# The transform's fp32 matmuls as two column tiles, the filter's as row tiles, and the filter's sums four channels at a time

## The chip, the cores and the metric

The kernel runs on one core of a Trainium2 chip. The metric is the device time of one execution in microseconds (us), lower is better. TensorE (PE) multiplies, and loads its stationary operands through a path that the profile lists as PEld; VectorE (DVE), ScalarE (ACT) and GpSimd (POOL) do the elementwise work, and SyncE (SP) issues most transfers.

## The reference

```python
h_mlp  = np.maximum(pos_emb @ w1, 0.0) @ w2            # (12480, 64) -> (12480, 128)
h_filt = h_mlp * np.exp(-0.01 * pos)[:, None]
Uf = np.fft.rfft(x * v, n=2 * S, axis=1)               # x, v: (2, 12480, 128)
Hf = np.fft.rfft(h_filt, n=2 * S, axis=0)
y  = np.fft.irfft(Uf * Hf[None], n=2 * S, axis=1)[:, :S]
x  = (x * y).reshape(24960, 128)
h = x @ w_in;  x = (h * np.cos(h)) @ w_out             # 128 -> 2048 -> 128
h = x @ w2_in; out = (h * np.clip(h + 3, 0, 6) / 6) @ w2_out
```

A long convolution with a filter that a small network makes from positions, then two wide layers in a row. Everything is fp32.

## The kernel before, in words

All work of a core stands in the order in which the code is written; nothing reorders it but the semaphores.

**Filter.** The 114 columns of positions are handled as two halves (`M2` = 57) stacked on the partitions: rows 0 to 63 hold the first half's features, rows 64 to 127 the second's. `mlp(k)` multiplies a chunk of four columns by a block-diagonal `w1b` (fp32) into `rp`; ACT makes its ReLU `rh` rounded to fp32r, DVE the rest `rl`. `filt(k)` multiplies each column with a block-diagonal `w2` in three fp32r products (`rh`·`w2h`, `rh`·`w2l`, `rl`·`w2h`) of 256 columns into `hps`; ACT copies a part of it (`raw`) for POOL, and POOL and DVE multiply by the window into `h`. There are 15 chunks.

**Transform.** The convolution of length 111 × 113 is done two channels at a time (`CH`), 64 iterations of the loop over `i`. A stage `s1(i, g)` multiplies 4 stationary blocks of 121 columns (two kinds, at columns 0 to 56 and 64 to 120, `OD` = 64) with the 112 columns of `f1` into `ap`; group 0 and 1 are the two batches' `uf`, group 2 the filter's `hf`. Two ACT copies (L269, L270) bring it to `at`: the lower half as it is, the upper half with its two parts exchanged. `s2h` and `s2u` (`xh`, `xp`) finish the forward transform, DVE multiplies (`pq`, `y`), `s2i` (`bp`) and `s1i` (`v`) go back, DVE forms `w`, and `fin` on POOL makes `z`, which is stored to DRAM. Each iteration of the loop holds stages of several `i`. For one `i + 2` POOL also makes `q` and, in `make_hf`, one product `hm` and four small sums (`hf`), for which the filter `h` lies in SBUF.

**The two layers** (`moe_phase`) run after the convolution with fp32r matmuls of 512 columns; a decoder in the loop prepares their weights.

An fp32 matmul of the code appears in the trace as two records, each with a weight load of its own; an fp32r matmul as one.

Of the kernel before, what the change touches and what calls it, by code (L numbers as in the profile page):

```python
# [22 lines left out]
R = 64  # L23
# [20 lines left out]
def kernel(  # L44
# [109 lines left out]
    def conv_phase(cctx):  # L154
# [18 lines left out]
        uf = [const.tile([N1, B, 2, CH, 128], FP32, name=f"uf{k}") for k in range(2)]  # L173
        hf = [const.tile([N1, 2, CH, 128], FP32, name=f"hf{k}") for k in range(2)]
        for k in range(2):
# [46 lines left out]
        def make_u(i, parts=(0, 1, 2)):  # L222
# [8 lines left out]
            for part, o, op in ((1, 0, ALU.add), (2, OD, ALU.subtract)):  # L231
                if part in parts:
                    nc.vector.tensor_tensor(out=f[:, :, o:o + M2], in0=pf, in1=qf, op=op)

        def make_hf(i):
            if i >= NG:
                return
            hm = p_u.tile([N1, CH, MP], FP32, tag="hm", name="hm")
            h = h_of(i * CH, CH)

            def sums(s_, t):
                for o, op in ((0, ALU.add), (OD, ALU.subtract)):
                    nc.gpsimd.tensor_tensor(
                        out=hf[i % 2][:, s_, :, o:o + M2], in0=t[:, :, :M2], in1=t[:, :, M2:], op=op
                    )

            if i < 2:
                sums(0, h)
            nc.gpsimd.tensor_tensor(
                out=hm, in0=h, in1=sig[:N1].unsqueeze(1).to_broadcast([N1, CH, MP]), op=ALU.mult  # L250
            )
            if i >= 2:
                sums(0, h)
            sums(1, hm)


        def s1(i, g, pool=None):
            if i >= NG:
                return
            if i not in a_t:  # L260
                a_t[i] = p_2.tile([KE, 2, 12, K1], FP32, tag="at", name="at")
            at = a_t[i]
            ap = (pool or ps_a).tile([KE, 4, 2, K1], FP32, tag="a", name="ap")
            for q in range(4):
                s, c = divmod(q, CH)
                st = (uf[i % 2][:, g, s, c] if g < 2 else hf[i % 2][:, s, c])[:, :KE]
                nc.tensor.matmul(out=ap[:, q].rearrange("p z k -> p (z k)"), lhsT=st, rhs=f1)  # L267
            src = ap.rearrange("p q z k -> p z q k")
            nc.scalar.copy(at[:OD, :, 4 * g:4 * g + 4, :], src[:OD])  # L269
            nc.scalar.copy(at[OD:, ::-1, 4 * g:4 * g + 4, :], src[OD:])  # L270

        with ExitStack() as hctx:
            hp = hctx.enter_context(tc.tile_pool(name="hp", bufs=1))
            hr = hctx.enter_context(tc.tile_pool(name="hr", bufs=3))
# [18 lines left out]
            nc.vector.memset(idle, 0.0)  # L293
            busy = ps_a.tile([128, 4 * NP1], FP32, tag="a", name="busy")
            for _ in range(2):
# [7 lines left out]
            for k in range(2, 8):  # L303
                load_pos(k)
            nc.vector.tensor_copy(w2h, w2s)
            nc.vector.tensor_tensor(out=w2l, in0=w2s, in1=w2h, op=ALU.subtract)
            rt = {}

            def mlp(k):
                n = chunks[k][1]  # L310
                rp = ps_r.tile([128, CB, NP1], FP32, tag="rp", name="rp")
                nc.tensor.matmul(out=rp[:, :n], lhsT=w1b, rhs=pt.pop(k)[:, :n])
                rh = hr.tile([128, CB, NP1], F32R, tag="rh", name="rh")
                rl = hr.tile([128, CB, NP1], F32R, tag="rl", name="rl")
                nc.scalar.activation(out=rh[:, :n], in_=rp[:, :n], func=ACTF.Relu)
                nc.vector.scalar_tensor_tensor(
                    out=rl[:, :n], in0=rp[:, :n], scalar=0.0, in1=rh[:, :n], op0=ALU.max, op1=ALU.subtract
                )
                rt[k] = (rh, rl)

            def filt(k):
                c0, n = chunks[k]
                rh, rl = rt.pop(k)
                hps = ps_h.tile([N1, CB, 2, D], FP32, tag="hps", name="hps")
                raw = hr.tile([N1, CB, 2, D - HS[2]], FP32, tag="raw", name="raw")
# [3 lines left out]
                nc.scalar.copy(raw[:, :n], hps[:, :n, :, HS[2]:])  # L329
                for e in range(2):  # L330
                    m = n
                    j0 = e * M2 + c0
                    nc.gpsimd.tensor_tensor(
                        out=h_p[2][:, :, j0:j0 + m].rearrange("p d c -> p c d"),
                        in0=raw[:, :m, e],
                        in1=win[:, j0:j0 + m].unsqueeze(2).to_broadcast([N1, m, D - HS[2]]),
                        op=ALU.mult,
                    )
                    for q, t in enumerate(h_p[:2]):
                        nc.vector.tensor_tensor(  # L340
                            out=t[:, :, j0:j0 + m].rearrange("p d c -> p c d"),
                            in0=hps[:, :m, e, HS[q]:HS[q + 1]],
                            in1=win[:, j0:j0 + m].unsqueeze(2).to_broadcast([N1, m, HS[q + 1] - HS[q]]),
                            op=ALU.mult,
                        )
# [81 lines left out]
        def s2i(i, g, pool=None):  # L427
            if not 0 <= i < NG:
                return
            if i not in b_t:  # L430
                if i < NG - 1:
                    b_t[i] = p_2.tile([2 * K1, 8, MP], FP32, tag="b", name="b")
                else:
                    t = p_2.tile([KE, 2, 12, K1], FP32, tag="at", name="bz").rearrange("p z q k -> p (z q k)")
                    b_t[i] = t[:2 * K1, :8 * MP].rearrange("p (a b) -> p a b", b=MP)
            src = (pool or ps_a).tile([2 * K1, 4, MP], FP32, tag="a", name="bp")
            for q in range(4):
                nc.tensor.matmul(out=src[:, q, :], lhsT=y_t[i][:, 4 * g + q, :], rhs=f2)  # L438
# [27 lines left out]
        def s1i_of(i, b, pool, tag):  # L466
            v = pool.tile([NP1, 2, 4, M2], FP32, tag=tag, name="vb")
            for z in (1, 0):
                nc.tensor.matmul(out=v[:, z], lhsT=gm[:, z, :], rhs=b_t[i][:, 4 * b:4 * b + 4, z * M2:(z + 1) * M2])
            vs = p_1.tile([NP1, 4, M2], FP32, tag=f"v2s{b}", name="v2b", bufs=3)  # L470
# [32 lines left out]
        for i in range(NG):  # L503
# [43 lines left out]
        def s1i_3(b):  # L547
            for z in (1, 0):
                nc.tensor.matmul(
                    out=vv[z][:, 4 * b:4 * b + 4], lhsT=gm[:, z, :],  # L550
                    rhs=b_t[n - 3][:, 4 * b:4 * b + 4, z * M2:(z + 1) * M2],
                )
            vs = p_1.tile([NP1, 4, M2], FP32, tag=f"v2s{b}", name="v2b", bufs=3)
# [276 lines left out]
def _constants():  # L830
# [75 lines left out]
```

## Time and profile before

| what | us |
|---|---|
| median of 3 runs (2753.46 to 2754.5) | 2754.06 |
| the profiled execution | 2752.64 |
| its span, first to last instruction | 2750.8 |
| filter, 4.44 to 38.09 | 33.65 |
| start of the loop, 38.09 to 62.04 | 23.95 |
| loop, i = 3 to 62, 62.04 to 537.54 (60 iterations) | 475.50 |
| end of the loop, 537.54 to 557.83 | 20.29 |
| the two layers, 557.83 to 2750.80 | 2192.97 |

The stretches are cut at first matmuls of a kind; the profiled execution takes 1.84 us more than its span, which lies before and after the instructions. PE is busy for 2733.3 us of the span (99%), PEld for 2199.1 (80%), DVE for 2349.4 (85%), ACT for 2273.1 (83%) and POOL for 2435.7 (89%). A matmul's busy time is longer than the distance to the next one, because matmuls are pipelined; where a rate is wanted, read distances between starts.

### The profile page before, as it was taken

Reading aid. Unit: us, or ns where it says so; the run is one execution under the profiler, and the core shown is the slowest. Engines: PE = TensorE matmul, PEld = TensorE weight load, DVE = VectorE, ACT = ScalarE, POOL = GpSimd, SP = SyncE. Lnnn points to the kernel's source line nnn. Section 1 sums busy time; section 2 is a strip of 40 time slices with the busy share of each in tenths; the row PEclk is TensorE's granted clock in tenths of the full one; section 3 lists DMA queues with packets and bytes.
Section 4 is the critical chain, followed back from the end, with each engine's and each line's share of the span. In section 5 each row is a group of like instructions: output and inputs, shape, how many; then the busy total and the mean of one; then the engine's idle time right before and its main releaser. Section 6 shows DMA issues by size and latency. Waiting matters only on the chain.

```text
span 2750.8 us, 39540 instructions
## 1 busy us (share of the span) xinstructions
PE 2733.3 (99%) x12965; PEld 2199.1 (80%) x12965; DVE 2349.4 (85%) x3199; ACT 2273.1 (83%) x3286; POOL 2435.7 (89%) x1544
## 2 busy tenths in 40 slices
PE   9999999989999999999999999999999999999999
PEld 7777777768888888888888888888888888888888
DVE  7888888778888888888888888888888888888887
ACT  5878777688888888888888888888888888888885
POOL 6999999788898889888988889888988888888887
PEclk9999999999999999999999999999999999999999
DMA  3333332200000000000000000000000000000000
GB/s 114 98 101 97 95 104 81 58 27 8 16 8 16 8 16 16 8 16 8 16 8 16 9 16 8 16 9 16 15 9 16 8 16 8 16 8 16 8 8 12
DMA packets 88288, 79.49 MB, mean 29 GB/s; under 512 B 57139, under 2 KB 78870, under 8 KB 88086
## 3 DMA queue, kind: packets, MB, share of 16 engines
q1 hardware_dynamic: 87790, 76.77, 10.2%
q8 instruction: 106, 1.74, 0.3%
q14 instruction: 96, 0.79, 0.1%
q10 hardware_dynamic: 296, 0.20, 0.0%
HBM read 51.19 MB, written 25.74 MB: 28 GB/s over the span
## 4 chain that ended last, share of the span: by engine, by line
PE 97%; ACT 1%; POOL 0%; DVE 0%; issue 0%; DMA 0%; SPq 0%; DVEq 0%; ACTq 0%
PE acc L733 39%; PE hb L665 20%; PE ha L665 19%; PE ap L267 6%; PE bp L438 4%; PE v L446 3%; PE xp L385 3%; PE xh L385 2%; POOL lo L698 0%; ACT r L685 0%; ACT k L675 0%; DMA x<-z 0%; DVE g L686 0%; ACT hi L693 0%; DVE r L676 0%
## 5 line engine op out<-in xcount | busy, mean ns | idle before, releaser
L723 POOL TENSOR_TENSOR lo<-g,hi 128x1024 fp32r<-128x1024 f32 (+1 forms) x390 | 938.8, 2407 | 238.9 <-PE ha L665 159.0
L698 POOL TENSOR_TENSOR lo<-g,hi 128x1024 fp32r<-128x1024 f32 (+1 forms) x392 | 942.0, 2404 | 3.4 <-ACT hi L693 2.7
L675 ACT ACTIVATE k<-ha,biasq 128x512 int32<-128x512 f32 (+1 forms) x768 | 509.1, 689 | 293.0 <-PE ha L665 292.8
L686 DVE TENSOR_TENSOR g<-ha,r 128x512 f32<-128x512 f32 (+1 forms) x768 | 500.1, 690 | 284.1 <-ACT r L685 283.9
L665 PE MATMUL hb<-x2h,vi 128*128 128x512 f32 (+1 forms) x1564 | 549.8, 392 | 0.0
L665 PE MATMUL ha<-xh,wi 128*128 128x512 f32 (+1 forms) x1524 | 535.5, 392 | 3.1 <-DVE g L686 3.0
L685 ACT ACTIVATE r<-r,biaspi 128x512 f32<-128x512 f32 (+1 forms) x776 | 520.3, 719 | 0.1
L676 DVE SCALAR_TENSOR_TENSOR r<-k,ha 128x512 f32<-128x512 int32 (+1 forms) x768 | 488.9, 677 | 2.9 <-ACT k L675 2.0
L706 DVE SCALAR_TENSOR_TENSOR g<-q,hb 128x1024 f32<-128x1024 f32 (+1 forms) x391 | 472.5, 1208 | 8.1 <-ACT q L705 8.1
L720 DVE SCALAR_TENSOR_TENSOR hi<-q,hb 128x1024 fp32r<-128x1024 f32 (+1 forms) x390 | 470.0, 1205 | 0.0
L705 ACT ACTIVATE q<-hb,bias 128x1024 f32<-128x1024 f32 (+1 forms) x391 | 435.3, 1113 | 20.5 <-PE hb L665 16.9
L733 PE MATMUL acc<-hi,vo 128*128 128x512 f32 (+1 forms) x1568 | 428.2, 395 | 0.0
L733 PE MATMUL acc<-hi,wo 128*128 128x512 f32 (+1 forms) x1568 | 427.7, 394 | 0.0
L693 ACT CAST hi<-g 128x1024 fp32r<-128x1024 f32 (+1 forms) x385 | 399.7, 1038 | 0.0
L733 PEld LDWEIGHTS acc<-hi,wo 128*128 128x128 f32 x1568 | 294.9, 188 | 71.4
L733 PEld LDWEIGHTS acc<-hi,vo 128*128 128x128 f32 x1568 | 294.3, 188 | 68.5
L665 PEld LDWEIGHTS hb<-x2h,vi 128*128 128x128 f32 x1564 | 293.7, 188 | 69.0 <-issue 0.4
L665 PEld LDWEIGHTS ha<-xh,wi 128*128 128x128 f32 x1524 | 286.2, 188 | 71.4 <-issue 3.1
L665 PE MATMUL hb<-x2l,vi 128*128 128x512 f32 (+1 forms) x782 | 306.5, 392 | 0.0
L665 PE MATMUL ha<-xl,wi 128*128 128x512 f32 (+1 forms) x762 | 303.9, 399 | 0.0
L733 PE MATMUL acc<-lo,wo 128*128 128x512 f32 (+1 forms) x784 | 247.7, 397 | 0.6 <-POOL lo L698 0.2
L733 PE MATMUL acc<-lo,vo 128*128 128x512 f32 (+1 forms) x784 | 245.8, 394 | 0.0
(144 smaller groups left out, 3402.1 us busy)
## 6 DMA issues: line engine op xcount, KB each, us to landing
x<-in_x_dram SPq DMA_DIRECT2D x64, 199.5 KB
v<-in_v_dram SPq DMA_DIRECT2D x64, 199.5 KB
scr<-z SPq DMA_DIRECT2D x128, 98.9 KB
out_dram<-o SPq DMA_DIRECT2D x47, 256.0 KB
xf<-scr SPq DMA_DIRECT2D x17, 256.0 KB
wst<-in_wi_dram SPq DMA_DIRECT2D x8, 512.0 KB
wst<-in_wo_dram SPq DMA_DIRECT2D x8, 512.0 KB
pt<-in_post_dram SPq DMA_DIRECT2D x14, 224.0 KB
```

The source lines that it names most:

```text
L665: nc.tensor.matmul(out=hs[c][:, 0, :n], lhsT=w["i", e][:, sl], rhs=r[:, :n], start=(k == 0), stop=(k == 2))
L675: nc.scalar.activation(out=k[:, c, :n], in_=h, func=ACTF.Identity, bias=biasq, scale=1.0 / TWO_PI)
L676: nc.vector.scalar_tensor_tensor(out=un.r[:, c, :n], in0=k[:, c, :n], scalar=-TWO_PI, in1=h, op0=ALU.mult, op1=ALU.add)
L685: nc.scalar.activation(out=rc, in_=rc, func=ACTF.Sin, bias=biaspi, scale=1.0)
L686: nc.vector.tensor_tensor(out=un.g[:, c, :n], in0=h, in1=rc, op=ALU.mult)
L693: nc.scalar.copy(un.hi[:, :, :n], un.g[:, :, :n])
L698: nc.gpsimd.tensor_tensor(out=un.lo[:, :, :n], in0=un.g[:, :, :n], in1=un.hi[:, :, :n], op=ALU.subtract)
L705: nc.scalar.activation(out=un.r[:, c, :n], in_=h, func=ACTF.Relu, bias=bias3, scale=1.0)
L706: nc.vector.scalar_tensor_tensor(out=un.g[:, c, :n], in0=un.r[:, c, :n], scalar=6.0, in1=h, op0=ALU.min, op1=ALU.mult)
L720: nc.vector.scalar_tensor_tensor(out=un.hi[:, c, :n], in0=un.r[:, c, :n], scalar=6.0, in1=h, op0=ALU.min, op1=ALU.mult)
L723: nc.gpsimd.tensor_tensor(out=un.lo[:, :, :n], in0=un.g[:, :, :n], in1=un.hi[:, :, :n], op=ALU.subtract)
L733: nc.tensor.matmul(out=acc[e][:, :n], lhsT=w["o", e][:, sl], rhs=r[:, c, :n], start=(u == 0 and c == 0 and k == 0), stop=(u == KFF // 2 - ...
```

## The change

**Column tiles.** A helper `mm` writes each matmul of the transform as two: stationary columns 0 to 63 into PSUM partitions 0 to 63, the others into partitions from 64 on. In `s1` the second one takes another moving operand, columns 56 to 167 of an `f1` to which a third block was added, so that the upper half comes out already exchanged, and one ACT copy of 121 partitions takes the place of the two.

**Row tiles.** In the filter `w2` is no longer block-diagonal: the first 64 partitions of `r` multiply with the first 64 of `w2s`, the other 64 with the other copy, in plain fp32, 128 columns each, into two PSUM tiles `hps0` and `hps1`. The split into `rh` and `rl` is gone. `mlp` is issued for two chunks at once, and the copies and products are ordered so that ACT and DVE start on different tiles.

**The filter's sums.** Every second iteration ACT copies four channels of `h` beside the place of their product with the signs (`hh`), POOL makes that product, and one sum and one difference of 456 elements cover four channels and both kinds; the difference is issued an iteration later. `hf` holds four channels. The first four channels still go the old way.

The idle matmuls at the start have 320 columns in place of 448.

```diff
-        f1 = const.tile([N1, 2 * K1], FP32, name="f1")
+        f1 = const.tile([N1, 3 * K1], FP32, name="f1")
...
+        def copy_h(m):
+            if HG * m < D:
+                hh_t[m] = p_u.tile([N1, 2, HG, MP], FP32, tag="hh", name="hh", bufs=1)
+                nc.scalar.copy(hh_t[m][:, 0], h_of(HG * m, HG))
+
+        def sums_h(m, parts):
+            if HG * m >= D:
+                return
+            hh, f = hh_t[m], hf[m % 2].rearrange("p s c n -> p (s c) n")
+            if 0 in parts:
+                nc.gpsimd.tensor_tensor(
+                    out=hh[:, 1], in0=h_of(HG * m, HG), in1=sig[:N1].unsqueeze(1).to_broadcast([N1, HG, MP]), op=ALU.mult
+                )
+            for part, o, op in ((0, 0, ALU.add), (1, OD, ALU.subtract)):
+                if part in parts:
+                    hf_sum(f[:, :, o:o + M2], hh.rearrange("p s c n -> p (s c) n"), op)
+
+
+        def mm(out, lhsT, rhs, rhs2=None):
+            m = lhsT.shape[-1]
+            nc.tensor.matmul(out=out[:OD], lhsT=lhsT[:, :OD], rhs=rhs)
+            nc.tensor.matmul(out=out[OD:m], lhsT=lhsT[:, OD:m], rhs=rhs if rhs2 is None else rhs2)
...
-                st = (uf[i % 2][:, g, s, c] if g < 2 else hf[i % 2][:, s, c])[:, :KE]
-                nc.tensor.matmul(out=ap[:, q].rearrange("p z k -> p (z k)"), lhsT=st, rhs=f1)
-            src = ap.rearrange("p q z k -> p z q k")
-            nc.scalar.copy(at[:OD, :, 4 * g:4 * g + 4, :], src[:OD])
-            nc.scalar.copy(at[OD:, ::-1, 4 * g:4 * g + 4, :], src[OD:])
+                st = (uf[i % 2][:, g, s, c] if g < 2 else hf[i // 2 % 2][:, s, i % 2 * CH + c])[:, :KE]
+                mm(ap[:, q].rearrange("p z k -> p (z k)"), st, f1[:, :2 * K1], f1[:, K1:])
+            nc.scalar.copy(at[:, :, 4 * g:4 * g + 4, :], ap.rearrange("p q z k -> p z q k"))
...
-                rh = hr.tile([128, CB, NP1], F32R, tag="rh", name="rh")
-                rl = hr.tile([128, CB, NP1], F32R, tag="rl", name="rl")
-                nc.scalar.activation(out=rh[:, :n], in_=rp[:, :n], func=ACTF.Relu)
-                nc.vector.scalar_tensor_tensor(
-                    out=rl[:, :n], in0=rp[:, :n], scalar=0.0, in1=rh[:, :n], op0=ALU.max, op1=ALU.subtract
-                )
-                rt[k] = (rh, rl)
+                r = rt[k] = hr.tile([128, CB, NP1], FP32, tag="r", name="r")
+                nc.scalar.activation(out=r[:, :n], in_=rp[:, :n], func=ACTF.Relu)
...
-                    for j, (l_, r_) in enumerate(((rh, w2h), (rh, w2l), (rl, w2h))):
-                        nc.tensor.matmul(out=hps[:, c], lhsT=l_[:, c, :N1], rhs=r_, start=(j == 0), stop=(j == 2))
...
+                    for e in range(2):
+                        h = slice(R * e, R * e + R)
+                        nc.tensor.matmul(out=hps[e][:, c], lhsT=r[h, c, :N1], rhs=w2s[h])
...
+                by_act(0)
+                by_dve(1)
+                by_act(1)
+                by_dve(0)
...
-                if k + 1 < len(chunks):
-                    mlp(k + 1)
+                for j in range(k + 2, min(k + 4, len(chunks))):
+                    if k % 2 == 0:
+                        mlp(j)
                 filt(k)
...
             for z in range(2):
-                nc.tensor.matmul(out=o[z], lhsT=cs[:, z, :], rhs=a[:, z, q0:q1, :])
+                mm(o[z], cs[:, z, :], a[:, z, q0:q1, :])
...
-                nc.tensor.matmul(out=src[:, q, :], lhsT=y_t[i][:, 4 * g + q, :], rhs=f2)
+                mm(src[:, q, :], y_t[i][:, 4 * g + q, :], f2)
...
-                nc.tensor.matmul(out=o, lhsT=gm[:, z, :], rhs=b[:, :, z * M2:(z + 1) * M2])
+                mm(o, gm[:, z, :], b[:, :, z * M2:(z + 1) * M2])
...
             make_p(i + 2)
+            if i % 2 or not i:
+                copy_h((i + 3) // 2)
             make_q(i + 2)
-            make_hf(i + 2)
+            sums_h((i + 3) // 2, (0, 1) if not i else (0,) if i % 2 else (1,))
```

On PE, one iteration of the loop before, from the filter's `s1` on (each row is one matmul of the code, `x4` four in a row; output <- moving, stationary; then the output's shape):

```order
L267 MATMUL ap<-f_88,hf_96 121x112 x4
L438 MATMUL bp<-f_89,y 112x114 x4
L267 MATMUL ap<-f_88,uf_94 121x112 x4
L438 MATMUL bp<-f_89,y 112x114 x4
L267 MATMUL ap<-f_88,uf_94 121x112 x4
L385 MATMUL xh<-at,cs 121x224 x2
```

On PE now, the end of the same part and what follows it in the iteration (`xh`, `xp`, `v`):

```order
L276 MATMUL xh<-at,cs 64x224
L277 MATMUL xh<-at,cs 49x224
L276 MATMUL xh<-at,cs 64x224
L277 MATMUL xh<-at,cs 49x224
L276 MATMUL xp<-at,cs 64x448
L277 MATMUL xp<-at,cs 49x448
L276 MATMUL xp<-at,cs 64x448
L277 MATMUL xp<-at,cs 49x448
L276 MATMUL v<-b,gm 64x456
L277 MATMUL v<-b,gm 48x456
```

The order of the stages stands; each matmul has become two, one for each column tile, with the same moving width.

On ACT, one iteration of the loop before (`at` from `s1`, `b` from `s2i`, `p` for DVE, `hs` from `s2h`, `v2s` from `s1i`):

```order
L269 COPY at<-ap 64x2x224
L270 COPY at<-ap 57x2x224
L439 COPY b<-bp 112x456
L269 COPY at<-ap 64x2x224
L270 COPY at<-ap 57x2x224
L439 COPY b<-bp 112x456
L269 COPY at<-ap 64x2x224
L270 COPY at<-ap 57x2x224
L220 COPY p<-x 111x2x114
L391 COPY hs<-xh 113x448
L449 COPY v2s<-v 112x456
```

On ACT now, an odd iteration:

```order
L291 COPY at<-ap 121x2x224
L461 COPY b<-bp 112x456
L291 COPY at<-ap 121x2x224
L461 COPY b<-bp 112x456
L291 COPY at<-ap 121x2x224
L223 COPY p<-x 111x2x114
L259 COPY hh<-h_85 111x456
L413 COPY hs<-xh 113x448
L471 COPY v2s<-v 112x456
```

Three copies of `at` are gone, and in odd iterations the copy of `h` stands between `p` and `hs`.

On POOL, one iteration before:

```order
L209 TENSOR_TENSOR q<-x,v 111x2x114
L212 TENSOR_TENSOR q<-q,sig 111x2x114
L249 TENSOR_TENSOR hm<-h_85,sig 111x228
L243 TENSOR_TENSOR hf_96<-h_85 111x2x57 x2
L243 TENSOR_TENSOR hf_96<-hm 111x2x57 x2
L461 TENSOR_TENSOR z<-w,sig 112x456
L462 TENSOR_TENSOR z<-z,w 112x456
L463 TENSOR_TENSOR z<-z,x 112x456
```

On POOL now, an odd iteration and the start of the even one after it:

```order
L212 TENSOR_TENSOR q<-x,v 111x2x114
L215 TENSOR_TENSOR q<-q,sig 111x2x114
L266 TENSOR_TENSOR hh<-h_85,sig 111x456
L239 TENSOR_TENSOR hf_95<-hh 111x8x57
L483 TENSOR_TENSOR z<-w,sig 112x456
L484 TENSOR_TENSOR z<-z,w 112x456
L485 TENSOR_TENSOR z<-z,x 112x456
L212 TENSOR_TENSOR q<-x,v 111x2x114
L215 TENSOR_TENSOR q<-q,sig 111x2x114
L239 TENSOR_TENSOR hf_95<-hh 111x8x57
```

Of five small operations in each iteration three large ones in every two are left.

## Rows read from the trace of the kernel before

**Rows 1.** The page, part 1: busy time, share of the span, instructions.

```profile
PE 2733.3 (99%) x12965; PEld 2199.1 (80%) x12965; DVE 2349.4 (85%) x3199; ACT 2273.1 (83%) x3286; POOL 2435.7 (89%) x1544
```

**Rows 2.** Busy time in stretches: length, each engine, clock, DMA share, GB/s.

```profile
core 0: us, PE busy (x) PEld busy (x) DVE busy (x) ACT busy (x) POOL busy (x), PEclk, DMA share, GB/s
...
4.44:38.09 33.65, 33.37 (x216) 27.07 (x214) 27.22 (x77) 16.75 (x33) 17.23 (x30) 1.00 0.48 142
...
62.04:537.54 475.50, 475.50 (x3121) 374.12 (x3120) 407.05 (x676) 370.16 (x721) 443.52 (x602) 1.00 0.34 91
...
557.83:2750.80 2192.97, 2183.16 (x9403) 1765.33 (x9401) 1887.04 (x2387) 1858.83 (x2480) 1939.60 (x838) 1.00 0.04 12
```

**Rows 3.** The chain that ended last, iteration i = 3: start, length, what.

```profile
62.20 0.84 PE ap L267 x8
63.04 0.79 PE bp L438 x8
...
66.31 0.76 PE xh L385 x4
67.07 1.50 PE xp L385 x4
68.57 1.55 PE v L446 x4
70.13 0.84 PE ap L267 x8
```

**Rows 4.** Groups by form, 62.04 to 537.54: count, busy us, mean ns, idle before.

```profile
L267 PE MATMUL ap<-f,uf 111*121 111x112 f32 x960 | 121.0, 269 | 0.0
...
L267 PEld LDWEIGHTS ap<-f,uf 111*121 111x121 f32 x960 | 111.1, 186 | 0.0
...
L270 ACT COPY at<-ap 57x448 f32<-57x448 f32 x180 | 95.0, 528 | 2.1
...
L463 POOL TENSOR_TENSOR z<-z,x 112x456 f32<-112x456 f32 x60 | 69.4, 1156 | 4.7
...
L461 POOL TENSOR_TENSOR z<-w,sig 112x456 f32<-112x456 f32 x60 | 65.7, 1095 | 20.9 <-DVE w L455 20.9
L439 ACT COPY b<-bp 112x456 f32<-112x456 f32 x120 | 64.7, 539 | 3.0
...
L243 POOL TENSOR_TENSOR hf<-h 111x114 f32<-111x114 f32 x116 | 47.1, 427 | 0.0
L249 POOL TENSOR_TENSOR hm<-h,sig 111x228 f32<-111x228 f32 x58 | 46.8, 806 | 0.0
L243 POOL TENSOR_TENSOR hf<-hm 111x114 f32<-111x114 f32 x116 | 43.2, 395 | 0.0
L385 PEld LDWEIGHTS xp<-at,cs 121*113 121x113 f32 x240 | 42.7, 178 | 25.1 <-issue 23.8
```

**Rows 5.** Waits, 62.04 to 537.54: total us, times, longest.

```profile
DVE p L228 <- ACT p L220: 55.7, 59, 1.5
```

**Rows 6.** Timeline of PE in the filter, one chunk and the next's start.

```profile
27.92 0.92 PE L312 MATMUL rp<-pt,w1b 128*128 128x448 f32 x2
...
29.07 0.28 PE L328 MATMUL hps<-w2h,rh 128*111 128x256 f32 x1
29.19 0.28 PE L328 MATMUL hps<-w2l,rh 128*111 128x256 f32 x1
...
30.12 0.91 PE L312 MATMUL rp<-pt,w1b 128*128 128x448 f32 x2
```

**Rows 7.** Timeline of POOL at the start of the loop.

```profile
45.77 0.63 POOL L249 TENSOR_TENSOR hm<-h,sig 111x228 f32<-111x228 f32 x1
...
47.05 0.74 POOL L243 TENSOR_TENSOR hf<-hm 111x114 f32<-111x114 f32 x2
```

**Rows 8.** The chain that ended last, start of the loop.

```profile
46.22 0.53 ACT at L270
...
50.95 0.54 ACT at L270
```

More of the change, by code (lines that the diff above doesn't have):

```diff
@@ L173, in conv_phase @@
         uf = [const.tile([N1, B, 2, CH, 128], FP32, name=f"uf{k}") for k in range(2)]
-        hf = [const.tile([N1, 2, CH, 128], FP32, name=f"hf{k}") for k in range(2)]
+        HG = 2 * CH
+        hf = [const.tile([N1, 2, HG, 128], FP32, name=f"hf{k}") for k in range(2)]
+        hh_t = {}
         for k in range(2):
@@ L233, in make_u, with hf_sum @@
                     nc.vector.tensor_tensor(out=f[:, :, o:o + M2], in0=pf, in1=qf, op=op)
+        def hf_sum(out, t, op):
+            nc.gpsimd.tensor_tensor(out=out, in0=t[..., :M2], in1=t[..., M2:], op=op)
         def make_hf(i):
-            if i >= NG:
-                return
[L238 to L244, printed above, removed]
-                    )
@@ L247, in make_hf @@
[L247 to L254, printed above, removed]
+            if not i:
+                hh_t[0] = p_u.tile([N1, 2, HG, MP], FP32, tag="hh", name="hh", bufs=1)
+            c = slice(i * CH, (i + 1) * CH)
+            h, hm = h_of(i * CH, CH), hh_t[0][:, 1, c]
+            for s_, t in enumerate((h, hm)):
+                if s_:
+                    nc.gpsimd.tensor_tensor(
+                        out=hm, in0=h, in1=sig[:N1].unsqueeze(1).to_broadcast([N1, CH, MP]), op=ALU.mult
+                    )
+                for o, op in ((0, ALU.add), (OD, ALU.subtract)):
+                    hf_sum(hf[0][:, s_, c, o:o + M2], t, op)
@@ L293, in conv_phase @@
             nc.vector.memset(idle, 0.0)
-            busy = ps_a.tile([128, 4 * NP1], FP32, tag="a", name="busy")
+            busy = ps_a.tile([128, 320], FP32, tag="a", name="busy")
             for _ in range(2):
@@ L321, in filt @@
+                nc.scalar.activation(out=r[:, :n], in_=rp[:, :n], func=ACTF.Relu)
             def filt(k):
                 c0, n = chunks[k]
-                rh, rl = rt.pop(k)
-                hps = ps_h.tile([N1, CB, 2, D], FP32, tag="hps", name="hps")
-                raw = hr.tile([N1, CB, 2, D - HS[2]], FP32, tag="raw", name="raw")
+                r = rt.pop(k)
+                hps = [ps_h.tile([N1, CB, D], FP32, tag=f"hps{e}", name=f"hps{e}") for e in range(2)]
+                raw = [hr.tile([N1, CB, D - HS[2]], FP32, tag=f"raw{e}", name=f"raw{e}", bufs=2) for e in range(2)]
@@ L339, in filt, with by_act, w, by_dve @@
+                def by_act(e):
+                    nc.scalar.copy(raw[e][:, :n], hps[e][:, :n, HS[2]:])
+                def w(e, m):
+                    return win[:, e * M2 + c0:e * M2 + c0 + n].unsqueeze(2).to_broadcast([N1, n, m])
+                def by_dve(e):
                     for q, t in enumerate(h_p[:2]):
                         nc.vector.tensor_tensor(
-                            out=t[:, :, j0:j0 + m].rearrange("p d c -> p c d"),
-                            in0=hps[:, :m, e, HS[q]:HS[q + 1]],
@@ L343, in filt @@
-                            in1=win[:, j0:j0 + m].unsqueeze(2).to_broadcast([N1, m, HS[q + 1] - HS[q]]),
-                            op=ALU.mult,
-                        )
+                            out=t[:, :, e * M2 + c0:e * M2 + c0 + n].rearrange("p d c -> p c d"),
+                            in0=hps[e][:, :n, HS[q]:HS[q + 1]], in1=w(e, HS[q + 1] - HS[q]), op=ALU.mult,
+                        )
+                by_act(0)
+                by_dve(1)
+                by_act(1)
+                by_dve(0)
@@ L347, in conv_phase @@
+                for e in range(2):
+                    nc.gpsimd.tensor_tensor(
+                        out=h_p[2][:, :, e * M2 + c0:e * M2 + c0 + n].rearrange("p d c -> p c d"),
+                        in0=raw[e][:, :n], in1=w(e, D - HS[2]), op=ALU.mult,
+                    )
             mlp(0)
+            mlp(1)
             for k in range(len(chunks)):
@@ L468, in s1i_of @@
             for z in (1, 0):
-                nc.tensor.matmul(out=v[:, z], lhsT=gm[:, z, :], rhs=b_t[i][:, 4 * b:4 * b + 4, z * M2:(z + 1) * M2])
+                mm(v[:, z], gm[:, z, :], b_t[i][:, 4 * b:4 * b + 4, z * M2:(z + 1) * M2])
             vs = p_1.tile([NP1, 4, M2], FP32, tag=f"v2s{b}", name="v2b", bufs=3)
@@ L548, in s1i_3 @@
             for z in (1, 0):
[L549 to L552, printed above, removed]
+                mm(vv[z][:, 4 * b:4 * b + 4], gm[:, z, :], b_t[n - 3][:, 4 * b:4 * b + 4, z * M2:(z + 1) * M2])
             vs = p_1.tile([NP1, 4, M2], FP32, tag=f"v2s{b}", name="v2b", bufs=3)
@@ L886 @@
         ("x", series(inputs["x"])), ("v", series(inputs["v"])), ("post", post.reshape(2 * R, M2, NP1)),
[L887 removed]
+        ("w1", twice(inputs["w1"])), ("w2", np.concatenate([inputs["w2"]] * 2)),
         ("wi1", bits(inputs["moe_w_in"])), ("wo1", bits(inputs["moe_w_out"])),
```

26 lines of the change are left out of this document (6 added, 20 removed).

## The prediction

> **What bounds the kernel now.** I read the table of busy shares first: PE 99%, the others 83 to 89% [rows 1]. Then the stretches, because the change touches only the filter and the convolution, some 558 us ahead of the two layers. In the 60 full iterations PE is busy for all of 475.50 us, POOL for 443.52, DVE for 407.05 and ACT for 370.16 [rows 2]. So PE sets the pace of the loop, 475.5 / 60 = 7.925 us an iteration, with POOL at 7.39, DVE at 6.78 and ACT at 6.17 behind it. The reader is to see that relief of ACT or POOL alone buys nothing here, and that a faster PE may win only some 7% before POOL as it is now would end last. In the filter PE is busy for 33.37 of 33.65 us [rows 2] and sets the pace too. The layers take 2192.97 us [rows 2], and no instruction of theirs changes; whatever is won before them I carry through whole.
>
> Next, what PE does with an iteration. The chain is PE all the way: three `ap` of 0.84 us, two `bp` of 0.79, `xh` 0.76, `xp` 1.50, `v` 1.55 [rows 3], together 7.91. `xp` has four records of 448 columns, 375 ns each or 0.837 ns a column. At this rate `ap` (8 records of 112) would take 94 ns a record and `bp` (114) 95, but they take 105 and 99. Over the 9024 columns of an iteration (24 records of 112, 16 of 114, 4 each of 224, 448 and 456) the pure stream is 7.55 us; 0.37 us are lost, 0.27 of it in `ap` and 0.05 in `bp`. The weight loads say why: in `ap` the loader has no idle time at all, in `xp` it waits 25.1 us over 240 loads [rows 4]. The short `ap` go at the pace of their loads of 121 columns, 0.87 ns a column.
>
> **Column tiles.** Cutting a matmul of 121 columns in two halves the columns, not the streaming: each half streams the whole moving operand, in two records. Alone this doubles the records to 104 an iteration. Upper bound: if nothing of one tile overlaps the other, the iteration takes twice 7.925 us, +475 us. Lower bound: if the tiles run beside each other, each tile streams the 7.55 us, and loads of 64 columns (56 ns at the same rate) hide behind streams of 94; that is -0.37 us times 60 = -22 us. No row shows two tiles at once. What stands nearest is that PE already keeps more than one short matmul in flight: one of `ap` lasts 269 ns [rows 4] and the next starts 105 ns after it. So I choose near the lower bound, and give back only what the loads cost in `ap` and `bp`: 0.32 x 60 = **-19 us**. By the Trainium skill (TensorEngine Tiling (Array Packing), Key Properties) tiles operate independently and can load weights and multiply in parallel; the sum by that is the same lower bound, and no trace here shows it yet.
>
> **ACT in the loop.** Of 360 copies of `at` 180 go, 95.0 us; each odd iteration gains one copy of 111x456, as `b` 539 ns [rows 4], some 30 x 0.54 = 16 us. ACT falls from 6.17 to 4.85 us an iteration. It costs and wins nothing by itself, for PE covers it. The new copy stands ahead of `hs`, but `p` and `hs` come out no later than before, since one copy of 528 ns ahead of them is gone. It waits for POOL's difference of the iteration before, nearly 8 us old.
>
> **POOL in the loop.** Removed: 47.1 + 46.8 + 43.2 = 137.1 us [rows 4]. Added, for every two iterations, a product of 456 elements (1.095 us, as `z` from `sig`) and two sums of 456 (1.156 each): 3.41 x 29 = 99 us. POOL falls from 7.39 to 6.75 us an iteration, under the 7.6 that PE would have. Without this the old 7.39 would still fit, barely; so this part too is worth nothing now and is cover for the first. An odd iteration has 1.095 + 1.156 of it, an even one 1.156, both no more than the 2.3 of before, so `hf` is no later.
>
> **Start of the loop.** At i = 0 POOL makes product, sum and difference for four channels at once: 3.41 us where the two channels took from 45.77 to 47.79, 2.0 us [rows 7], and the next iteration's first `s1` waits for it: up to +1.4. The chain there also has a second copy of `at` twice, 0.53 and 0.54 [rows 8], which go: -1.1. One lies behind the other only in part; I take **+0.5**, bounds -1.1 to +1.4.
>
> **Filter.** Two chunks take 2 x 2.20 = 4.40 us (27.92 to 30.12), of which 24 fp32r records of 256 columns at 117 ns [rows 6]. Afterwards: 4 records of `mlp` at 375 ns, 1.50, and 32 records of 128 columns at 107 ns. Side by side the row tiles take 16 x 107 = 1.71, in all 3.21: -1.19 for each of some 7 pairs, -8.3 us. One after the other 3.43, and the switch between two shapes of the array on top, twice a pair. No row prices such a switch; I bound it by nothing and by the time a matmul outlasts the next start, 269 - 105 = 164 ns. That gives 5.26 us, +6.0. I take overlap and the full switch, 3.54 us: **-6 us**. DVE, busy for 27.22 us here [rows 2], loses the `rl` operations and fits under the new 27.6; ACT and POOL, at about half, fit too. The shorter idle matmuls I leave at nothing.
>
> **Sum.** -19 - 6 + 0.5 = -24.5 on the profiled execution's 2752.64 gives 2728; the median stands 1.4 above that execution, so **2729**. The end of the loop (20.29 us) is a chain of many engines in which I see no term.
>
> **Rivals.** *Program order across tiles.* If a record that must wait for its own tile holds up everything behind it, of each matmul one record is alone with its partner, and one shares its place with the next matmul, as long as the longer of the two. Counting an iteration's stages so gives 4512 + 4860 columns, 7.84 us: -0.08 x 60 - 6 + 0.5, **2744**. For it: records leave PE in order; against it: nothing. The Trainium skill (TensorE: Matmul & The Clock Gate, Part 3, The mechanism) has matmuls start and end strictly in program order; this rival is what that does here.
>
> *Loads one at a time.* If one loader serves both tiles, an `ap` matmul loads 242 columns at 0.87 ns, 210 ns, just what it takes now; nothing is won in the loop, and the filter's 32 loads of 111 columns make 3.08 us in place of 1.71, +0.5 a pair. Then **2758**.
>
> *The records come too fast* (the rival on the other side). An iteration's 20 short matmuls become 80 pairs of load and matmul, in 4.10 us now. They may take 51 ns a pair before the loop loses, 52 with the filter's gain counted. The shortest pace in these rows is the 99 ns of `bp`, which would be +229 us; nothing shows that PE can start pairs at half of that. At 60 ns it is +0.70 x 60 = +42 us, and 1.5 less from the filter: **2792**. Against it: the 24 long records of a tile pair leave time to prepare others ahead. By the Trainium skill (TensorE: Matmul & The Clock Gate, Wait — 56ns, not 53.3ns?) decoding in software costs about 62 ns per matmul; by that figure the sum would be 2802, unless the queue evens it out over the iteration, in which 104 x 62 ns is 6.4 us.
>
> *No overlap at all*: +475 + 6, about **3235**. *Faster than the stream*, for a reason that I do not know: then DVE ends last, 6.78 us busy plus its wait for `p`, 55.7 / 60 = 0.93 [rows 5] less the 0.53 of the copy gone ahead of `p`: 7.18 us, -45 us, **2703**.
>
> **Numbers.** Overlap near the stream 0.47 (own range 2725 to 2738); program order 0.20; loads one at a time 0.09; records too fast 0.12; no overlap 0.05; faster than the stream 0.07. A change of 0.2%, 5.5 us, is about the least that a measurement of this kernel tells from none. Faster: 0.47 + 0.07 + most of program order, 0.16, is 0.70. Same: 0.04 of it and 0.06 of the loads, 0.10. Slower: 0.20. The range 2703 to 2762 holds the first three and the last, 0.83; the two slow cases above it stay out.
>
> **What would show it.** Iterations 7.6 us apart, with `ap` at 0.75 to 0.77 us a group and records of the two tiles starting nearly together; 7.84 with `xh`, `xp` and `v` longer by 0.3 in all means program order; `ap` still at 0.84 means loads; `ap` and `bp` above 0.84 with the loader idle means pairs too fast. Chunk pairs of the filter at 3.5 us, POOL at 6.75 and ACT at 4.85 us an iteration test the other terms. The prediction falls if `xp` takes more than 1.6 us, or if an engine other than PE ends last in the loop.

## The result and the profile after

The changed kernel took 2731.0 us (median of 4 runs, 2730.14 to 2732.04) against 2753.85 for the kernel before beside it (4 runs): a ratio of 0.9919 [0.9907, 0.9931], 22.9 us less. The forecast was 2729. Beside the experiments the kernel before took 2752.62, 2752.66 or 2753.22 us, so a difference of 1 or 2 us between two of the runs below tells little. One of the five executions of `e8_mlp_single` took 3351.71 us, at a granted clock of 0.75 where the others had 1.00, and is left out of its ratio. The page, part 1, against [rows 1]:

```profile
PE 2710.7 (99%) x16362; PEld 2149.7 (79%) x16362; DVE 2339.4 (86%) x3182; ACT 2184.6 (80%) x3140; POOL 2411.8 (88%) x1327
```

The same stretches as [rows 2] (filter, start, loop, end, layers), cut at the same first matmuls; the columns after the length are busy time and instructions of PE, PEld, DVE, ACT and POOL:

```profile
3.80:33.88 30.08, 28.93 (x286) 19.64 (x286) 19.48 (x64) 16.37 (x46) 18.68 (x32) 1.00 0.54 165
33.88:56.44 22.56, 20.15 (x255) 14.42 (x255) 14.44 (x29) 12.41 (x27) 17.26 (x28) 1.00 0.35 102
56.44:517.64 461.20, 461.20 (x6243) 337.64 (x6240) 406.04 (x676) 286.82 (x569) 419.56 (x398) 1.00 0.36 94
517.64:536.85 19.21, 16.70 (x181) 12.38 (x177) 12.86 (x29) 8.63 (x18) 13.39 (x18) 1.00 0.24 60
536.85:2728.50 2191.65, 2181.26 (x9403) 1764.45 (x9401) 1886.28 (x2387) 1858.93 (x2480) 1939.67 (x838) 1.00 0.04 12
```

The span became 22.3 us shorter. The filter is done 4.2 us sooner (33.88 for 38.09; 0.6 of it because its first matmul starts at 3.80 for 4.44), the start of the loop is shorter by 1.4, the loop by 14.3 of its 475.50 [rows 2], its end by 1.1 and the layers by 1.3. PE's timeline in an iteration (start, duration, record; L276 is the tile of 64 columns, L277 the other):

```profile
293.17 0.55 PE L277 MATMUL v<-b,gm 112*48 112x456 f32 x1
293.18 0.55 PE L276 MATMUL v<-b,gm 112*64 112x456 f32 x1
...
294.73 0.26 PE L277 MATMUL ap<-f,hf 111*57 111x112 f32 x1
294.74 0.26 PE L276 MATMUL ap<-f,hf 111*64 111x112 f32 x1
...
295.49 0.26 PE L277 MATMUL bp<-f,y 113*48 113x114 f32 x1
...
300.85 0.55 PE L277 MATMUL v<-b,gm 112*48 112x456 f32 x1
```

From `v` at 293.17 to `v` at 300.85 an iteration takes 7.68 us (it was 7.925). The two tiles' records start 0.01 us apart, in the long `v` and in the short `ap` alike, and an `ap` group takes 295.49 - 294.73 = 0.76 us in place of the 0.84 of [rows 3]. Groups of the loop, 56.44 to 517.64:

```profile
L291 ACT COPY at<-ap 121x448 f32<-121x448 f32 x180 | 95.8, 532 | 40.1 <-PE ap L277 33.8 <-PE ap L276 6.3
...
L239 POOL TENSOR_TENSOR hf<-hh 111x456 f32<-111x456 f32 x58 | 57.9, 999 | 23.9 <-issue 19.5 <-POOL hh L266 3.2
L215 POOL TENSOR_TENSOR q<-q,sig 111x228 f32<-111x228 f32 x58 | 57.8, 997 | 4.6
...
L266 POOL TENSOR_TENSOR hh<-h,sig 111x456 f32<-111x456 f32 x28 | 35.9, 1283 | 0.0
```

One copy of 121 rows takes the 0.53 us that each of the two copies took [rows 4]. But `q` (228 elements) has a mean of 997 ns, almost that of a sum twice as long. That is the trace of something I had not counted, as the runs show.

### The profile page after: what moved, and what is told of

Same layout as the page of the kernel before. It is cut to its first block, busy times and chain, and to the rows that moved or that the text cites. A ratio compares the mean times of both kernels' runs of the same rounds, so it can differ in the third digit from the quotient of the medians.

```text
span 2728.5 us, 45720 instructions
## 1 busy us (share of the span) xinstructions
PE 2710.7 (99%) x16362; PEld 2149.7 (79%) x16362; DVE 2339.4 (86%) x3182; ACT 2184.6 (80%) x3140; POOL 2411.8 (88%) x1327
## 4 chain that ended last, share of the span: by engine, by line
PE 98%; ACT 1%; POOL 0%; DVE 0%; issue 0%; DMA 0%; ACTq 0%; DVEq 0%; POOLq 0%
PE acc L754 40%; PE hb L686 20%; PE ha L686 19%; PE ap L277 5%; PE v L277 3%; PE xp L277 3%; PE bp L277 3%; PE xh L277 2%; PE ap L276 1%; PE rp L329 0%; PE hps L342 0%; PE bp L276 0%; ACT r L706 0%; ACT k L696 0%; POOL hf L239 0%
```

## The experiments

In short: **tiles** are the column tiles, **sums** the filter's sums for four channels at a time, **filter** the filter's matmuls as row tiles and what goes with them.

**1 to 4: one part away, or one part alone.**

`e1_no_col`, the changed kernel without column tiles:

```diff
-            nc.tensor.matmul(out=out[:OD], lhsT=lhsT[:, :OD], rhs=rhs)
-            nc.tensor.matmul(out=out[OD:m], lhsT=lhsT[:, OD:m], rhs=rhs if rhs2 is None else rhs2)
+            nc.tensor.matmul(out=out, lhsT=lhsT, rhs=rhs)
```

(and the two copies of `at` for the one.)

> The changed kernel with its column tiles undone alone: each matmul of the transform whole again, two copies of at again; row tiles and the new sums stay. My theory (the loop won because loads of short stationary blocks hide in column tiles): the iteration goes back from 7.69 to about 7.92 us, the total to 2745 to 2748 us, and the filter keeps its 5 us. Rival (the loop won by the relief of ACT or POOL): most of the gain stays, iteration below 7.8 us, total below 2739 us.

Measured: 2749.98 us, 0.9986 [0.9977, 0.9996]. The chain that ended last (start, length, what) is back at the old pace:

```profile
297.78 0.84 PE ap L289 x8
...
305.71 0.31 PE ap L289 x3
```

305.71 - 297.78 = 7.93 us. So filter and sums without tiles are worth 2.6 us, and the tiles on top of them 19.0 (2749.98 to 2731.0; 20.2 when each is taken against the kernel before beside it).

`e2_old_sums`, the changed kernel with the product and sums of before (two channels at a time, `hm` and four sums):

```diff
-            sums_h((i + 3) // 2, (0, 1) if not i else (0,) if i % 2 else (1,))
+            make_hf(i + 2)
```

> The changed kernel with the filter's sums as before (product of two channels and four sums an iteration on POOL, no copy by ACT). My theory (PE ends last, POOL at 7.4 us is cover): the same as the changed kernel, 2730 to 2733 us, iteration 7.69 us, POOL busy over 96% of the loop. Rival (with PE faster, POOL ends last): iteration 7.75 us or more, total 2735 us or more, PE waits for POOL's hf or DVE's w.

Measured: 2746.59 us, 0.9977 [0.9968, 0.9985]: only 6 us of 22.9 are left, though the tiles are in. PE's timeline, the first `v` of successive iterations and what PE waited for between (in brackets):

```profile
301.13 0.55 PE L260 MATMUL v<-b,gm 112*64 112x456 f32 x1
...
308.82 0.55 PE L260 MATMUL v<-b,gm 112*64 112x456 f32 x1
...
311.08 0.41 PE L260 MATMUL ap<-f,hf 111*64 111x112 f32 x2 [0.36 <-POOL hf L244]
...
317.73 0.56 PE L260 MATMUL v<-b,gm 112*64 112x456 f32 x1
```

One iteration takes 7.69 us, the next 8.91: PE waits for POOL's `hf`. This goes on in threes between 204 and 406 us (7.69, 7.69, 8.91), 8.10 in the mean, worse than the 7.925 of before. Three is the number of iterations that the decoder gives to a piece of the weights. The timeline of POOL and of DVE at the long one:

```profile
304.94 1.16 POOL L468 TENSOR_TENSOR z<-z,w 112x456 f32<-112x456 f32 x1
306.18 2.57 POOL L469 TENSOR_TENSOR z<-z,x 112x456 f32<-112x456 f32 x1
...
305.29 1.16 DVE L461 TENSOR_TENSOR w<-v,v2s 112x456 f32<-112x456 f32 x2
306.37 0.69 DVE L126 SCALAR_TENSOR_TENSOR wmh<-wst,wmh 128x512 f32<-128x512 uint32 x1
306.97 0.42 DVE L114 TENSOR_SCALAR wex<-wst 128x512 int32<-128x512 int32 x1
307.31 0.42 DVE L115 TENSOR_SCALAR wmh<-wst 128x512 int32<-128x512 int32 x1
307.76 0.40 DVE L229 TENSOR_TENSOR p<-p,v 111x228 f32<-111x228 f32 x1
```

`z<-z,x` takes 2.57 us where its twin takes 1.16: 1.41 more. DVE is in three operations of the decoder from 306.37 to 307.76, 1.39 us. POOL seems to stand while they run; runs 10 to 12 ask that.

`e3_col_only`, the kernel before with the column tiles alone:

> The kernel before with the column tiles alone (and the one copy of at that they allow). My theory: iteration 7.69 us, 14 to 16 us less than before in all, 2737 to 2740 us. Rival (tiles pay only together with POOL's relief): iteration above 7.75 us, total above 2743 us.

Measured: 2751.76 us, 0.9997 [0.9988, 1.0005], no change that can be told. The loader's wait says why (the group that loads `hf`, 100 to 450 us):

```profile
L259 PEld LDWEIGHTS ap<-f,hf 111*64 111x64 f32 x352 | 36.3, 136 | 20.7 <-POOL hf L243 14.0 <-issue 1.8 <-POOL z L464 0.3
```

With tiles alone PE's loads wait for POOL's `hf`, 17.8 us over both tiles; without tiles they do not. POOL is busy for 339.6 of these 350 us, and gaps of 0.08 us between its operations make up the other 10.5: as it was it could not follow.

`e4_load128`, the kernel before with 7 more (unread) columns in each `ap` load, 128 for 121:

```diff
-[:, s, c])[:, :KE]
+[:, s, c])
```

> The kernel before, whose s1 loads stationary blocks of 128 columns (the last seven are zero, their results are not read) in place of 121; streams and copies as they were. My theory (these matmuls go at the pace of the weight loads, 0.87 ns a column): ap from 105 to 111 ns a record, 24 x 6 = 0.15 us an iteration, 9 us more, 2762 to 2764 us. Rival (105 ns is a fixed cost of a short record, whatever is loaded): the same as before, 2752 to 2756 us.

Measured: 2762.16 us, 1.0035 [1.0023, 1.0048]. In the chain a group of `ap` takes 0.88 and 0.89 us for the 0.84 of [rows 3]:

```profile
296.61 0.88 PE ap L267 x8
297.50 0.79 PE bp L438 x8
298.28 0.89 PE ap L267 x8
```

8 loads of 7 columns at 0.87 ns are 0.049 us. So the short `ap` of before did go at the pace of their loads.

**5 to 8: the matmuls.**

`e5_tile_order`: in each group first all records of the tile of 64 columns, then all of the other (the second matmul is put in a list, which is emptied at the end of the group).

> The changed kernel with another order of the same matmuls: in each group first all of tile 0, then all of tile 1 (for ap and bp four and four, for the long ones two and two). Theory A (each tile works off records of its own, PE looks far enough ahead): unchanged, 2730 to 2736 us. Theory B (a record that waits for its tile holds up all behind it): tile 1 always lies one group behind tile 0, a slot lasts as long as the longer of two neighbouring groups, 8.5 us an iteration, some 50 us more, 2775 to 2790 us. A value between means that PE looks ahead only a few records.

Measured: 2765.03 us, 1.0043 [1.0029, 1.0057], between the two theories. PE's timeline in `v` (L277 now the first tile, L283 the second):

```profile
302.67 0.54 PE L283 MATMUL xp<-at,cs 121*49 121x448 f32 x1
302.72 0.56 PE L277 MATMUL v<-b,gm 112*64 112x456 f32 x1
303.05 0.56 PE L283 MATMUL v<-b,gm 112*48 112x456 f32 x1
303.12 0.55 PE L277 MATMUL v<-b,gm 112*64 112x456 f32 x1
```

The first tile's `v` runs beside the second's `xp`, and the second's first `v` (303.05) starts before the first's second (303.12). So the tiles do not start in program order, in which the first tile has all four `v` before the second's first. But an iteration (`v` at 302.72 and at 310.93) takes 8.21 us, 0.52 more than where the two alternate. I read it as the first tile getting ahead only by a long record or a few short ones; what holds it was not tried.

`e6_four_tiles`: four tiles of up to 32 columns for the two, 208 records an iteration.

> The changed kernel with four column tiles of 32 in the transform in place of two of 64: the same streams side by side, twice the records and loads. If pairs of load and matmul have no least distance above 24 ns, the iteration stays at 7.69 us, 2730 to 2735 us. Rival of the prediction (records come too fast), with the limit between 24 and the 48 ns that the changed kernel shows: the 20 short matmuls of an iteration take 160 pairs; at 40 ns that is 6.4 in place of 3.9 us, 2.5 us an iteration, 150 us more.

Measured: 2734.43 us, 0.9933 [0.9919, 0.9947], 3.4 us above the changed kernel (4.1 when each is taken against the kernel before beside it). At 96 / 4 = 24 ns a record the pairs of load and matmul are still not too fast; the forecast's rival needed a limit of over 51.

`e7_s1_only`: column tiles for `ap` alone, so that PE changes between one tile and two six times an iteration.

```diff
+            if rhs2 is None:
+                nc.tensor.matmul(out=out, lhsT=lhsT, rhs=rhs)
+                return
```

> The changed kernel with column tiles in s1 alone; bp, xh, xp and v are whole matmuls again, so that the shape of the array changes six times an iteration. If a change of shape costs nothing: about 2732 us. At the 0.16 us that I put in for the filter: 6 x 0.16 = 1 us an iteration, 60 us more, 2785 to 2800 us.

Measured: 2794.1 us, 1.0148 [1.0132, 1.0163]. PE's timeline:

```profile
301.40 0.31 PE L279 MATMUL ap<-f,hf 111*64 111x112 f32 x1
301.41 0.30 PE L280 MATMUL ap<-f,hf 111*57 111x112 f32 x1
...
302.32 1.04 PE L277 MATMUL bp<-f,y 113*112 113x114 f32 x8
303.29 0.31 PE L279 MATMUL ap<-f,uf 111*64 111x112 f32 x1
```

`ap` to `bp` takes 0.92 us and `bp` to `ap` 0.97, for 0.76 and 0.79 without a change. An iteration takes 8.68 us (`v` at 291.08 and 299.76). The old 7.925 less three `ap` at 0.07 is 7.72; the other 0.96 is 0.16 for each of six changes.

`e8_mlp_single`: the filter's chunks one at a time, so twice the changes of shape.

> The changed kernel with mlp issued for one chunk at a time, as before the change, in place of two: two more changes of shape for every two chunks, some 14 in all. At 0.16 us each: 2.3 us more, 2732 to 2735 us. If a change of shape costs nothing: 2730 to 2732 us.

Measured: 2732.3 us, 0.9926 [0.9913, 0.994]. The time hardly moves: 1.3 us, which these runs cannot tell from none. In the trace a chunk takes 2.01 us (starts of `hps` at 8.92 and 10.93); a pair, 4.02, against 3.63 in the changed kernel, is 0.39 for two more changes, about 0.2 each.

**9 to 12: POOL.**

`e9_filter_only`, the kernel before with the new filter alone (tiles undone as in the first run, sums as in the second):

> The kernel before with the new filter alone (no column tiles, the old sums). Theory A: the filter's gain is the 5 us by which its end comes sooner, whatever runs behind it, so 2747.5 to 2749; the new sums without the tiles then cost 1 to 2 us against it, at the loop's start, where the tensor engine waits 1.5 us for them in the kernel with both. Theory B: the sums cost nothing at the start and the filter alone is worth no more than filter and sums together: 2749.5 to 2750.5.

Measured: 2748.24 us, 0.9984 [0.9975, 0.9993], in the range of theory A. With the first two runs the square is full (all with the new filter):

| | one matmul | column tiles |
|---|---|---|
| old sums | 2748.24 | 2746.59 |
| new sums | 2749.98 | 2731.0 |

The sums alone cost 1.7 us and the tiles alone win 1.7, neither of which these runs can tell from none; the two together win 17.2 (18.4 when each is taken against the kernel before beside it).

`e10_no_masks`, `e2_old_sums` without three operations of the decoder on DVE (L114, L115, L130; ACT reads the words unmasked, so the masking is left out of the decoded weights):

```diff
-        nc.vector.tensor_scalar(ex, hi, 9, 0x3FFFFF, op0=ALU.logical_shift_right, op1=ALU.bitwise_and)
-        nc.vector.tensor_scalar(mh, hi, 0x1FF, None, op0=ALU.bitwise_and)
...
-        nc.vector.tensor_scalar(ex, ex, -0x800000, None, op0=ALU.bitwise_and)
```

> The changed kernel with the old sums (2746.6), and three of the decoder's operations on the vector engine left out (L114, L115, L130: masks and a shift with one input, 0.42 us each, 16 tasks), so that the weights decoded are wrong. Theory A: GpSimd is the engine that ends last there, and it stands still while these three run, 16 x 1.25 = 20 us in all: without them GpSimd falls under the tensor engine's pace and the time comes to that of the changed kernel or a little above it, 2731 to 2737. Theory B: GpSimd's long operations have another cause: 2745 to 2747.

Measured: 2732.23 us, 0.9926 [0.9913, 0.9938]. With the old sums the time is that of the changed kernel but for 1.2 us, and an iteration takes 7.69 us (`v` at 293.32, 301.00, 308.69). POOL's groups, 100 to 450 us:

```profile
L466 POOL TENSOR_TENSOR z<-z,x 112x456 f32<-112x456 f32 x46 | 53.3, 1159 | 3.6
...
L241 POOL TENSOR_TENSOR hf<-hm 111x114 f32<-111x114 f32 x90 | 43.0, 500 | 0.0
```

`z<-z,x` is at 1159 ns, from 1542 in `e2_old_sums`. `hf<-hm` is at 500, from 391: it now meets L119 and L124, the decoder's operations with two inputs, which are left in.

`e11_masks_twice`: `e2_old_sums` with those three operations done twice each.

> The changed kernel with the old sums, and the same three operations done twice over (48 more operations of 0.42 us on the vector engine, which has idle time). Theory A: GpSimd, full already, stands still for up to 20 us more: 2760 to 2767. Theory B: the vector engine's own idle time takes them: 2746 to 2749.

Measured: 2766.1 us, 1.0048 [1.0035, 1.006], in the range of theory A, but not by its way alone: POOL now also waits 20.1 us for DVE's `w` (100 to 450 us), DVE's masks take up to 1.18 us in the mean in place of 0.42, and PE's granted clock has a mean of 0.98.

`e12_after_masks_twice`: the changed kernel with the three done twice.

> The changed kernel itself with the three operations done twice. Theory A: GpSimd has 461 - 420 = 41 us to spare in the loop since its sums became fewer, and the 20 us of standing fit into them: 2731 to 2734. Rival: each stand delays an operation that the tensor engine waits for, so that part of the 20 us shows: 2738 to 2750.

Measured: 2775.44 us, 1.0083 [1.007, 1.0097]. Both theories missed it. Groups of 100 to 450 us, of POOL, PE and DVE:

```profile
L486 POOL TENSOR_TENSOR z<-w,sig 112x456 f32<-112x456 f32 x40 | 50.1, 1251 | 29.3 <-DVE w L480 29.3
...
L279 PE MATMUL ap<-f,uf 111*64 111x112 f32 x656 | 86.4, 276 | 22.3 <-DVE uf L239 22.3
...
L117 DVE TENSOR_SCALAR wmh<-wst 128x512 int32<-128x512 int32 x13 | 15.4, 1183 | 0.4
```

The second mask of a pair (L117) takes 1183 ns for 0.42: now DVE stands for POOL. DVE is busy for 339.4 of 350 us, and PE waits for its `uf`, seven times for 3.2 us. After each of these waits its granted clock falls for a while to 0.5, that is 1.2 of 2.4 GHz; the mean over the 350 us is 0.96, where the changed kernel has 1.00, so up to 14 of the 44 us (0.04 of 350, an estimate) are the clock and not the waits themselves. The timeline of POOL and DVE at one piece shows them taking turns:

```profile
276.39 1.70 POOL L215 TENSOR_TENSOR q<-x,v 111x228 f32<-111x228 f32 x1
278.17 0.71 POOL L218 TENSOR_TENSOR q<-q,sig 111x228 f32<-111x228 f32 x1
...
276.54 0.68 DVE L128 SCALAR_TENSOR_TENSOR wmh<-wst,wmh 128x512 f32<-128x512 uint32 x1
277.14 0.42 DVE L114 TENSOR_SCALAR wex<-wst 128x512 int32<-128x512 int32 x1
277.59 0.80 DVE L115 TENSOR_SCALAR wex<-wst 128x512 int32<-128x512 int32 x1
```

POOL's `q` (0.68 elsewhere) is 1.02 longer, the 0.60 and 0.42 of L128 and L114; then L115 takes 0.80. My 41 us to spare was wrong too: in 100 to 450 us of the changed kernel POOL is busy for 332.3 and loses 10.8 in gaps that no wait explains, so only 7 of 350 us are free.

## Why the prediction was right, and where it was not

**The time and the chosen case.** 2731.0 for 2729, by the way that was chosen: the tiles overlap, and PE sets the pace of the loop. The rivals' conditions fell one by one. Program order: records of the two tiles start 0.01 us apart in every stage, and with the tiles' order changed they still start out of program order (303.05 before 303.12). The rule of the Trainium skill that stood beside this rival (TensorE: Matmul & The Clock Gate, Part 3, The mechanism), that matmuls start strictly in program order, does not hold across tiles here. Loads one at a time: `ap` came down to 0.76 us. Records too fast: 24 ns a record is no limit. No overlap: refuted by the time itself. Faster than the stream: no; the records keep 0.84 to 0.86 ns a column. That the sum came within 2 us is in part luck. The loop and the filter's end gave 4.7 and 1.8 us less than their terms, the start, the end and the layers together 4.3 more; and more than half of the gain hung on a part that was priced at nothing and happened to be in the change.

**Column tiles, -19.** On top of the other parts they made 19.0 us (2749.98 to 2731.0), but not as reckoned. The 60 iterations gave 14.3: 7.69 us each for the forecast's 7.6. Some 2 ns of each of the 52 pairs of records over the pure stream were not won, 0.1 us an iteration: `ap` goes at 96 ns for 94, `bp` at 97.5 for 95. That is the loop's term, right in mechanism and too large by 4.7 us. The rest lies outside the 60 iterations, where the forecast gave the tiles nothing. The loop's first matmul comes at 59.87 us in `e1_no_col` and at 56.44 with the tiles, 3.4 sooner: 1.1 in the filter and 2.4 in the start of the loop (24.92 to 22.56). Another 2.4 us are in the layers, which have no tiles; there the clock differs (**End and layers** below). Without that the tiles are worth some 17 us, an estimate.

**POOL, "cover".** This step failed. The prediction said that POOL's old 7.39 us "would still fit, barely; so this part too is worth nothing now". It did not fit: with the old sums 15.6 of the 22.9 us are gone (some 1.9 of them by the clock in the layers), and the tiles alone are worth nothing that can be told. The new sums are not a spare cover: more than half of the gain hangs on them. Two things were wrong in the 7.39. It is the mean over a stretch that holds 20.9 us of waits of POOL [rows 4], 7.9 of them at its start and 12.9 after 450 us, when the decoder is done. Between 100 and 450 us the kernel before shows:

```profile
100.00:450.00 350.00, 350.00 (x2293) 274.89 (x2292) 305.58 (x512) 278.73 (x541) 339.57 (x458) 1.00 0.36 98
...
L212 POOL TENSOR_TENSOR q<-q,sig 111x228 f32<-111x228 f32 x44 | 44.6, 1014 | 3.5
```

POOL is busy for 339.6 of 350 us, and the remaining 10.5 are gaps of 0.08 us after three of its operations. So it was full at 7.925, tied with PE, and no share of busy time over the whole loop shows that. And part of this busy time is standing: about 0.6 us an iteration (`q` with a mean of 1014 ns and `hm` with 862, where they take 635 and 631 in `e10_no_masks`, are 27 us over 44 iterations). Taking three of the decoder's operations from DVE alone brought the time from 2746.59 to 2732.23, so this standing was what POOL lacked. The same is left in the changed kernel: POOL is busy for 419.56 / 60 = 6.99 us an iteration, where the forecast had 6.75.

That it is an exclusion between DVE and POOL and not mere slowness is shown by both directions, POOL's operation longer by just DVE's time in `e2_old_sums` and DVE's masks longer in the last run. The Trainium skill has this rule (SBUF — State Buffer, Who interferes with whom): GpSimd shares a pair of ports with DVE, an instruction of DVE in a two-port mode or with two inputs in SBUF contends for it, and whoever issues first holds it for the whole instruction while the other stands. The traces agree that the two exclude each other: L126 has two inputs in SBUF; DVE's operations with an input in PSUM (`w`, `p`) leave POOL's at 1.16. They do not show that the first holds: `z<-z,x` starts at 306.18, before L126 at 306.37, and is the one that stands. Why the single masks made POOL stand while the doubled ones stand themselves is not settled; I read it as the second mask, which waits for the first on the same tile, letting POOL in between, and did not test that.

**Filter, -6.** Alone it is worth 4.4 us. A pair of chunks takes 3.63 us for the forecast's 3.54:

```profile
11.45 2.00 PE L342 MATMUL hps<-w2s,r 64*111 64x128 f32 x32
13.38 1.77 PE L329 MATMUL rp<-pt,w1b 128*128 128x448 f32 x4
15.08 2.00 PE L342 MATMUL hps<-w2s,r 64*111 64x128 f32 x32
```

(PE's timeline in the changed kernel.) The price of a change of shape was at the upper end of its bounds, 0.164 us, or above it: run 7 gives 0.16, run 8, in the filter itself, 0.2. Some of the last chunks run singly, and PE is busy for only 28.93 of the 30.08 us, where it was for 33.37 of 33.65 [rows 2]; the forecast counted on PE alone.

**Start, +0.5.** The stretch became shorter, by 1.4 us. What the forecast feared is there: with the new sums alone PE waits 1.53 us for them, and the loop's first matmul comes at 59.87 us (`e1_no_col`) for 58.78 with the old ones (`e9_filter_only`), 1.1 us later, inside the upper bound of 1.4. The second set of sums ends at 46.15 us there, for 44.53. The tiles, which the term left out, more than made up for it. The clock explains little of it, though it is low for a part of this stretch in the kernel before: `e4_load128`, at 1.00 throughout, takes 24.02 us for it without tiles, and `e12_after_masks_twice`, at a mean of 0.92, takes 22.56 with them.

**ACT, nothing.** ACT is busy for 286.82 us, 4.78 an iteration (4.85 forecast). What its relief is worth by itself was not tried.

**End and layers.** 1.1 and 1.3 us less; the forecast carried both through unchanged. Why the end is shorter no run asked. In the layers no instruction changed, but PE's granted clock did. After waits of PE of 2.71 and 2.42 us it falls from 1.00 to 0.5 (2.4 to 1.2 GHz) twice in the kernel before, and after one of 2.66 us once in the changed kernel; the rows give the mean of each stretch:

```profile
557.00:561.00 4.00, 4.00 (x14) 3.57 (x13) 2.47 (x4) 3.23 (x5) 0.12 (x1) 0.57 0.30 68
594.50:598.50 4.00, 4.00 (x11) 3.14 (x12) 2.78 (x4) 3.46 (x5) 4.00 (x2) 0.57 0.00 0
```

```profile
544.50:548.00 3.50, 3.50 (x12) 3.08 (x11) 2.70 (x4) 2.70 (x5) 3.17 (x2) 0.52 0.00 0
```

(The kernel before, then the changed one; the last column but two is the clock.) The other runs fit: from the first `ha` to the end the layers take 2193.8 to 2194.2 us with one such stretch (also `e6_four_tiles`, `e12_after_masks_twice`), 2194.9 to 2195.6 with two, 2195.7 and 2195.9 where one of two lasts about twice as long (`e2_old_sums`, `e7_s1_only`), 2196.2 with three (`e1_no_col`, `e4_load128`). So the 1.3 us go with the clock and not with work that the change took away. Whether the change or chance made it fall less often is not shown.

## What to carry to other kernels

Before a part of a change is called cover and priced at nothing, take the busy time of the engine that it relieves from the densest stretch, not from the whole loop, and add the small gaps that no wait explains: an engine at 97% there is full. Compare an operation's mean with its median (over the changed kernel's loop `q` has 997 and 637 ns); where the mean is half as much again, look at what another engine does at the long ones. And of a change in two parts on two engines that are tied, neither part shows its worth alone: only the square of the four versions does. Before a difference of 1 or 2 us is put down to a part of the change, compare the granted clock in the stretches that the change leaves alone.

## What the runs showed of the hardware

- Two column tiles cost nothing in records: 104 an iteration (208 with four tiles, 24 ns apart) keep the pace of the stream, 0.86 ns a column in records of 112. The two tiles' records may start out of program order; issued group by group the second tile ran 0.33 us behind the first, and an iteration took 0.52 us longer (`e5_tile_order`).
- A change between one tile and two (or between 128 rows and two tiles of 64) costs 0.16 to 0.2 us each; six of them an iteration turned a gain into +1.5%.
- A matmul's load that is longer than its stream sets the pace: 0.87 ns a column loaded, so 7 more columns in each load of `ap` cost 9.5 us in all (`e4_load128`).
- One operation of 1.16 us on GpSimd took 2.57 beside three of DVE's, with one or two inputs in SBUF; done twice, DVE's second mask took 1.18 for 0.42 in the mean.
- A stretch of low clock in the layers (0.5 for 1.00, after a wait of PE) cost some 1.2 us of the kernel: 2193.8 us with one, 2195.0 with two.
